# Weight-preparation buffers, operand loads and modulation gradients moved in a one-core adaLN transformer-block backward kernel

## The chip, the cores and the metric

The kernel runs on 1 core of one Trainium2 chip. The metric is device time in microseconds (us) of one launch. Five runs before the change gave 2850.62, 2851.59, 2852.38, 2853.69 and 2855.15 us; their median is 2852.38 us.

The core has a matrix engine (PE, with its own weight loads, PEld), a vector engine (DVE), an activation engine (ACT), a general engine (POOL, called GpSimd in the code) and a queue engine (SP, called `nc.sync`). SP and POOL also issue DMA transfers. All transfers run on the core's 16 DMA engines. Every engine takes its instructions strictly in order: an instruction that waits holds up all that are behind it on the same engine.

## The reference

The reference is the forward pass of one block and its gradients for ten tensors. S = 2048 rows, D = 512, F = 1792, 32 heads of 16.

```python
mod = (_silu(c) @ w_mod).reshape(c.shape[0], 6, 1, -1)     # sa, ca, ga, sb, cb, gb
h = _layernorm(x, axis=-1) * (1 + ca) + sa
x = x + ga * _A_ref(h, A_wqkv, A_wo)          # softmax attention
h = _layernorm(x, axis=-1) * (1 + cb) + sb
x = x + gb * _B_ref(h, B_w1, B_b1, B_w2, B_b2)   # squared-relu MLP
...
_out, _vjp = jax.vjp(_f, A_x, A_wqkv, A_wo, B_w1, B_b1, B_w2, B_b2, c, w_mod)
_grads = _vjp(grad_out)
```

The kernel returns the block's output (`out_0`), then the gradients of `A_x` (`out_1`), `A_wqkv` (`out_2`), `A_wo` (`out_3`), `B_w1`, `B_b1`, `B_w2`, `B_b2` (`out_4` to `out_7`), `c` (`out_8`) and `w_mod` (`out_9`). The last is 512 x 3072: six blocks of 512 columns, one for each of the six modulation vectors.

## The kernel before

The program has four stretches.

1. **Forward attention with the MLP beside it** (`phase_fwd`, L243): to about 1110 us.
2. **The last MLP chunk and the MLP's weight gradients** (`last_chunk`, L558). The weight gradients are generators that give one unit of work for each large matmul (`gen_dw1`, `gen_dw2`), driven by a `Background` object: `take(n)` runs n units, `until(mark)` runs up to a mark, `drain()` runs the rest. `gen_dw2` (L791) computes dW2 in 14 blocks, `ft` = 0 to 13, of 16 matmuls each. Block `ft` needs the transposed activations `a_blk` of that block, which SP loads with a transposing DMA (L802) from `aT_d` in HBM. `a_blk` has three buffers, and the load for block ft+2 is issued when block ft begins, so a load needs the buffer of the block three before. After each block DVE scales and reduces the result (L819, L822), POOL stores it (L820) and accumulates (L823). After block 7 the generator gives the mark "half", then does 16 matmuls for dB2 (L828), then blocks 8 to 13.
   At the mark "half" SP is given two other jobs, between the remaining `a_blk` loads:
   - `load_bwd` (L1102): 11 transfers ("pieces") that attention backward needs for its first head group: four of keys and values (128 KB each), four of QT and dOT (256 KB each), three of K, Q and dO (256 KB each).
   - `load_wmt` (L1108): four rounds, one for each 128 rows of `A_wqkv`. In a round SP loads the rows into `w_kt` (L1115, 384 KB), ACT scales them (L1116), and SP transposes them into `WmT` (L1118), the weights with which the last stretch computes dx. `w_kt` has one buffer, so the load of a round waits until the transpose of the round before has read it; the transpose waits for ACT, which waits for the load. `last_chunk` takes 13 units of dW2 at each of the eight stops of this generator.
3. **Attention backward** (`attn_bwd`, L1149): 1024 steps (8 head groups x 2 head pairs x 4 key chunks x 16 query blocks), 1250 to about 2707 us. A step does score matmuls (L1265), dP matmuls (L1218), exponentials on ACT (L1269), a product on DVE (L1223), and sends ds through a transposing DMA on SP (L1227, `dsT`) for the dQ matmuls (L1199).
4. **dx, the attention's weight gradients and the modulation gradients** (`phase6`, L1291): four generators, joined in one loop. `gen_a` (16 row tiles, 12 matmuls each) makes dx; its operand `dqT` comes through SP: `load_a` (L1323) issues three transposing DMAs (L1327) and one plain load (L1330) for a pair of row tiles, with two buffers, so a load waits until the pair two before is done. `gen_b` makes dWqkv: three column sums (L1355), then 12 blocks of 16 matmuls (L1368) into two PSUM buffers `g3ps`; DVE reads each result twice (L1373, L1376), and POOL stores it (L1374, two buffers `dwq`). `gen_c` makes dWo (L1393). `gen_p7` makes the gradients of `w_mod` and `c`, one vector `j` at a time in the order 3, 4, 5, 2, 0, 1: POOL loads 512 KB of `w_mod` into `wmod7` (L1434), PE broadcasts the vector (L1446), ACT copies it to `dm7` (L1448), DVE and ACT make the outer product `dwm7` (L1454, L1456), SP stores it (L1457, 512 KB), and DVE reduces against `wmod7` in four operations (L1460). `wmod7`, `dm7` and `dwm7` have one buffer each, so the load for the next j waits until this j's four reductions are done.
   The loop runs `gen_b` eight times, then rounds of c, b, a and, where its inputs are there, one j: j = 3, 4, 5 in rounds 1 to 3; j = 2 when c is done; j = 0 and 1 when b is done.

In stretches 1 to 3 the order on PE and SP is that of the code (`manual_schedule`, L142), and the order on the other engines comes from a planner that works on estimated times. In stretch 4 the planner orders all engines.

Of the kernel before, what the change touches and what calls it, by code (L numbers as in the profile page):

```python
# [8 lines left out]
BF16 = mybir.dt.bfloat16  # L9
# [9 lines left out]
P = 128  # L19
# [14 lines left out]
class Background:  # L34
# [13 lines left out]
    def next(self):  # L48
        while self.gens:
            r = next(self.gens[0], None)  # L50
            if r is not None:
                if isinstance(r, tuple):
                    self.mark = r[0]
                    self.seen.add(r[0])
                return r
            self.gens.pop(0)
        return None
# [30 lines left out]
class K:  # L88
# [469 lines left out]
    def last_chunk(self, bg, O_b, x0s):  # L558
# [5 lines left out]
        nc, io, mk, mps = self.nc, self.io, self.mk, self.mps  # L564
        D, F, H, NQ, ST, DT, FT, SC = self.D, self.F, self.H, self.NQ, self.ST, self.DT, self.FT, self.SC
        sc, s0, st0 = SC - 1, 512 * (SC - 1), 4 * (SC - 1)
        tm_v = lambda t: t.rearrange("(st p) d -> p st d", p=P)[:, st0:st0 + 4, :]
        tps = self.open_pool("tps", bufs=2, space=PSUM)
        e0 = self.open_pool("e0", bufs=1)
# [71 lines left out]
        fill = Background()  # L641
# [76 lines left out]
        next(g2)  # L718
        self.open_bwd()
        fill.until("half")  # L720
        self.load_bwd()
        for _ in self.load_wmt():
            fill.take(13)
        fill.drain()
        for name in ("dw2", "dw1", "e0", "dwps", "tps", "mps"):
            self.close_pool(name)

    def gen_dw1(self, sb, xh2):
# [370 lines left out]
                nc.vector.memset(m, 0.0)  # L1099
        self.qp = self.open_pool("p5q", bufs=1, side="right")  # L1100

    def load_bwd(self):  # L1102
        nc = self.nc
        self.T0, pieces = self.load_group(0)
        for (d, sr) in self.pair_pieces(0, 0) + pieces:
            nc.sync.dma_start(d, sr)

    def load_wmt(self):  # L1108

        nc, io = self.nc, self.io  # L1110
        D, DT = self.D, self.DT
        self.WmT = self.wp.tile([P, 3 * DT, D], BF16, name="WmT")
        for kt in range(DT):
            w = self.wp.tile([P, 3 * D], BF16, name="w_kt")
            nc.sync.dma_start(w[:], io["A_wqkv"][kt * P:(kt + 1) * P, :])  # L1115
            nc.scalar.activation(w[:], w[:], ACT.Copy, scale=self.opcaT[:, kt:kt + 1])  # L1116
            yield
            nc.sync.dma_start_transpose(self.WmT[:, :, kt * P:(kt + 1) * P], w[:])  # L1118
            yield

    def load_group(self, g):

# [168 lines left out]
    def phase6(self):  # L1291

        tc, nc, pp, io = self.tc, self.nc, self.pp, self.io
        S, D, H, ST, DT = self.S, self.D, self.H, self.ST, self.DT
# [8 lines left out]
        with ExitStack() as es:  # L1303
            sb = es.enter_context(tc.tile_pool(name="p6", bufs=1))
# [28 lines left out]
            def gen_a():  # L1333
                nxt = load_a(0)
                for s2 in range(0, ST, 2):
                    dqT, dx1 = nxt
                    if s2 + 2 < ST:
                        nxt = load_a(s2 + 2)
                    for k in range(2):
                        st = s2 + k  # L1340
                        pt = ps_a.tile([P, 512], F32, name="dxhps")
                        for nt in range(NT):
                            nc.tensor.matmul(pt[:], lhsT=dqT[:, nt // DT, k, nt % DT, :], rhs=WmT[:, nt, :],
                                             start=(nt == 0), stop=(nt == NT - 1))
                        dx0 = wk.tile([P, D], BF16, name="dx0")
                        self.ln_bwd_tile(wk, pt[:], xhat1[:, st, :], dx1[:, k, :], self.rstd1[:, st:st + 1], dx0[:])
                        nc.gpsimd.dma_start(out1_v[:, st, :], dx0[:])  # L1347
                        yield
# [57 lines left out]
            ga, gb, gc, g7 = gen_a(), gen_b(), gen_c(), self.gen_p7(sb, ob7, ps7)  # L1406
            want = next(g7)
            done = set()

            def run(name, gen):  # L1410
                if name not in done and next(gen, "done") == "done":
                    done.add(name)

            for _ in range(8):
                run("b", gb)
            while len(done) < 3 or want is not None:
                run("c", gc)
                run("b", gb)
                run("a", ga)
                if want is not None and (want in (3, 4, 5) or (want == 2 and "c" in done) or "b" in done):  # L1420
                    want = next(g7, None)
# [3 lines left out]
    def gen_p7(self, sb, ob, ps, order=(3, 4, 5, 2, 0, 1)):  # L1425
        tc, nc, pp, io = self.tc, self.nc, self.pp, self.io
        D, DT = self.D, self.DT
        wmod_v = io["w_mod"].rearrange("(kt p) n -> p kt n", p=P)
        dc_part = sb.tile([P, DT, 6], F32, name="dc_part")
        nc.gpsimd.memset(dc_part[:], 0.0)  # L1430
        for j in order:
            yield j
            wmod = ob.tile([P, DT, D], BF16, name="wmod7")
            nc.gpsimd.dma_start(wmod[:], wmod_v[:, :, j * D:(j + 1) * D])  # L1434
            cols = {0: self.dsa_col, 1: self.dca_col, 3: self.dsb_col, 4: self.dcb_col}
            if j == 2:
                dm = self.dga_bc
            else:
                if j == 5:
                    dg = self.dgb_acc  # L1440
                else:
                    dg = ob.tile([P, D], F32, name="dg7")
                    for kt in range(DT):
                        nc.vector.tensor_scalar(dg[:, kt * P:(kt + 1) * P], self.ident_f[:], cols[j][:, kt:kt + 1], None, ALU.mult)
                pt = ps.tile([P, 512], F32, name="bcps")
                nc.tensor.matmul(pt[:, :D], lhsT=self.ones_f[:], rhs=dg[:], start=True, stop=True)  # L1446
                dm = ob.tile([P, D], F32, name="dm7")
                nc.scalar.copy(dm[:], pt[:, :D])  # L1448
            if "dmod_bc" in self.dbg:
                nc.sync.dma_start(self.dbg["dmod_bc"][:, j * D:(j + 1) * D], dm[:])  # L1450
            o = ob.tile([P, DT, D], BF16, name="dwm7")
            for kt in range(DT):
                if kt % 2 == 0:
                    nc.vector.tensor_scalar(o[:, kt, :], dm[:], self.scT[:, kt:kt + 1], None, ALU.mult)  # L1454
                else:
                    nc.scalar.activation(o[:, kt, :], dm[:], ACT.Copy, scale=self.scT[:, kt:kt + 1])  # L1456
            nc.sync.dma_start(io["out_9"].rearrange("(kt p) n -> p kt n", p=P)[:, :, j * D:(j + 1) * D], o[:])  # L1457
            for kt in range(DT):
                junk = ob.tile([P, D], F32, name="junk7")
                nc.vector.scalar_tensor_tensor(junk[:], wmod[:, kt, :], 1.0, dm[:], ALU.mult, ALU.mult,  # L1460
                                               accum_out=dc_part[:, kt, j:j + 1])
        yield -1
        dcT = sb.tile([P, DT], F32, name="dcT")
        nc.vector.tensor_reduce(dcT[:], dc_part[:], axis=AX.X, op=ALU.add)
        nc.vector.tensor_tensor(dcT[:], dcT[:], self.dsiluT[:], ALU.mult)
        pt = ps.tile([P, 512], F32, name="bcps")
        nc.tensor.transpose(pt[:DT, :P], dcT[:], self.ident_f[:])
        dc_b = sb.tile([DT, P], BF16, name="dc_b")
        nc.vector.tensor_copy(dc_b[:], pt[:DT, :P])
        nc.sync.dma_start(io["out_8"].rearrange("o (t p) -> (o t) p", p=P), dc_b[:])  # L1470
# [73 lines left out]
```

The softmax here doesn't subtract the row's maximum and nothing guards it: scores larger than these inputs give would overflow.

## Time and profile before

One execution was profiled. It took 2850.62 us as a run, and its span from the first to the last instruction is 2848.8 us, so 1.8 us lie around the span.

| what | value |
|---|---|
| median of five runs | 2852.38 us |
| profiled execution, as a run | 2850.62 us |
| its span | 2848.8 us |
| PE busy | 2540.2 us, 89% of the span |
| ACT busy | 2214.7 us, 78% |
| DVE busy | 1786.4 us, 63% |
| POOL busy | 362.5 us, 13% |
| mean granted PE clock | 0.961 of full speed |
| first score matmul of attention backward (L1265) | 1250.18 us |
| last matmul of attention backward | about 2718 us |
| DMA share, 1200 to 1250 us | 0.97 |
| DMA share, 2700 to 2750, 2750 to 2800, 2800 to 2849 us | 0.94, 0.65, 0.76 |

How to read the views used below. A line of the timeline has the start in us, the length, the engine, the source line, the operation with output<-inputs, and the count of instructions merged into it. A bracket at its end gives how long the engine stood idle before it and what released it. SPq is SP as it issues DMAs; its length is the time for which the issue held the queue, not the transfer. A line of the waits view has who waited for whom, the total in us, the number of times, and the longest. The DMA share is the busy share of the 16 DMA engines and can pass 1.

### The profile page before, as it was taken

To read this page: it belongs to the slowest core of one execution; us is meant where nothing else is said; L and a number is where in the kernel's file an instruction comes from. 1 tells how busy PE (TensorE), PEld (TensorE's weight loads), DVE (VectorE), ACT (ScalarE), POOL (GpSimd) and SP (SyncE) were. 2 spreads that over 40 slices of the span, in tenths; PEclk is the share of its full clock that TensorE was granted. 3 is DMA by queue.
4 is the path that set the end of the run, shared out by engine and by line. 5 is a ranking of instruction groups with operands and counts; after the bars stand their busy time and mean duration, and the time that the engine had idled before them with its cause. 6 is when DMAs were issued, how large, how long until landed. Compare 5 with 4: busy or idle time off the path is not lost. (4 is left out here: it accounts for less than half of the span.)

```text
span 2848.8 us, 72467 instructions
## 1 busy us (share of the span) xinstructions
PE 2540.2 (89%) x30186; PEld 1214.3 (43%) x30186; DVE 1786.4 (63%) x2712; ACT 2214.7 (78%) x3376; POOL 362.5 (13%) x633
## 2 busy tenths in 40 slices
PE   5999799999999999978888888898988889888887
PEld 2555455555555545723333333333333333333343
DVE  4222423323312345658888888888988989889747
ACT  4999899999999975247778777777877878778623
POOL 2244202211311123420000000000000000000021
PEclk9999999999999999989999999999999999999899
DMA  4367743520531356989999999999999999999977
GB/s 150 86 148 161 166 78 100 122 53 29 144 86 45 100 151 176 196 194 201 212 196 204 207 200 210 196 203 204 195 208 200 201 207 199 208 201 207 213 192 187
DMA packets 1331345, 472.86 MB, mean 166 GB/s; under 512 B 1266470, under 2 KB 1293608, under 8 KB 1331016
## 3 DMA queue, kind: packets, MB, share of 16 engines
q1 hardware_dynamic: 1299816, 379.40, 72.6%
q0 software_dynamic: 29088, 86.21, 10.3%
q8 instruction: 236, 3.87, 0.5%
q10 hardware_dynamic: 2112, 2.62, 0.3%
q14 instruction: 93, 0.76, 0.1%
HBM read 83.30 MB, written 67.11 MB: 53 GB/s over the span
## 5 line engine op out<-in xcount | busy, mean ns | idle before, releaser
L1269 ACT ACTIVATE pu<-st 128x512 bf16<-128x512 f32 x2048 | 1109.0, 595 | 312.9 <-PE dp L1218 283.7
L1223 DVE TENSOR_TENSOR ds<-dp,pu 128x1024 bf16<-128x1024 f32 x1024 | 1213.2, 1219 | 195.7 <-PE dp L1218 155.8
L331 ACT ACTIVATE pu<-st 128x1024 bf16<-128x1024 f32 x1024 | 955.5, 1044 | 23.0 <-PE st L328 21.5
L328 PE MATMUL st<-QTm,KTq 128*128 128x512 bf16 x2048 | 608.7, 378 | 28.7 <-ACT pu L331 7.0
L293 PEld LDWEIGHTS <-pu 128*128 128x128 bf16 x8192 | 344.4, 96 | 246.4 <-issue 20.2
L1265 PE MATMUL st<-m,q 64*128 64x512 bf16 x1024 | 370.0, 402 | 19.0 <-ACT pu L1269 8.6
L1265 PE MATMUL st<-m,QTq 64*128 64x512 bf16 x1024 | 365.5, 398 | 15.9 <-ACT pu L1269 4.5
L1199 PEld LDWEIGHTS <-dsT 128*128 128x128 bf16 x8192 | 240.9, 97 | 309.4 <-DMA dsT<-ds 194.8
L1218 PE MATMUL dp<-m,q 64*128 64x512 bf16 x1024 | 371.9, 406 | 0.0
L1218 PE MATMUL dp<-m,dOTq 64*128 64x512 bf16 x1024 | 367.3, 402 | 0.0
L293 PE MATMUL accbank<-Vaug,pu 128*128 128x17 bf16 x8192 | 348.8, 171 | 13.6 <-DVE O L301 12.8
L328 PEld LDWEIGHTS <-KTq 128*128 128x128 bf16 x2048 | 194.4, 96 | 205.8 <-issue 140.5
L1199 PE MATMUL accq<-Kg,dsT 128*128 128x16 bf16 x4096 | 143.6, 171 | 81.6 <-DMA dsT<-ds 81.6
L1199 PE MATMUL accq<-q,dsT 128*128 128x16 bf16 x4096 | 144.3, 171 | 70.5 <-DMA dsT<-ds 70.2
L1434 POOL DMA_DIRECT2D wmod<-in_w_mod_dram x6 | 4.6, 774 | 1459.8 <-DVE kvT L1182 1453.6
L1179 PE MATMUL acckv<-ds,q 128*16 128x512 bf16 x1024 | 163.7, 402 | 0.0
L1179 PE MATMUL acckv<-pu,q 128*16 128x512 bf16 x1024 | 163.7, 402 | 0.0
L1179 PE MATMUL acckv<-ds,Qg 128*16 128x512 bf16 x1024 | 162.8, 400 | 0.7 <-DVE ds L1223 0.7
L1179 PE MATMUL acckv<-pu,dOg 128*16 128x512 bf16 x1024 | 162.9, 400 | 0.0
L1218 PEld LDWEIGHTS <-q 64*128 64x128 bf16 x1024 | 90.5, 94 | 111.4 <-issue 102.1
L1218 PEld LDWEIGHTS <-dOTq 64*128 64x128 bf16 x1024 | 89.4, 94 | 102.4 <-issue 93.6
L300 DVE RECIPROCAL rl<-accbank 128x4 f32<-128x4 f32 x128 | 22.9, 179 | 164.8 <-PE accbank L293 164.6
(309 smaller groups left out, 2372.3 us busy)
## 6 DMA issues: line engine op xcount, KB each, us to landing
KTq<-KTq_d POOLq DMA_DIRECT2D x24, 512.0 KB, 3.7
duT_d<-auT POOLq DMA_DIRECT2D x4, 1792.0 KB, 8.3
aT_d<-rT POOLq DMA_DIRECT2D x4, 1792.0 KB, 13.4
KTq_d<-KTq SPq DMA_DIRECT2D x32, 128.0 KB, 1.8
QTq_d<-ev_fm SPq DMA_DIRECT2D x32, 128.0 KB, 2.3
VTq_d<-vT POOLq DMA_DIRECT2D x4, 1024.0 KB, 6.2
O_d<-O POOLq DMA_DIRECT2D x4, 1024.0 KB, 5.4
m<-KTq_d SPq DMA_DIRECT2D x32, 128.0 KB, 3.6
```

The costliest lines, as they stand in the source:

```text
L293: nc.tensor.matmul(acc[:, a, sub, :], lhsT=pu[:, a, sub * P:(sub + 1) * P], rhs=Vaug[:, kb, h, :], start=(kb == 0 and a == 0 and sub == 0) ...
L300: nc.vector.reciprocal(self.rl[:, st0:st0 + 4, h], acc[:, a, :, DH])
L328: nc.tensor.matmul(stt[:, a, :], lhsT=KT[:, kb * P:(kb + 1) * P], rhs=QTm[2 * jp + a][:], start=True, stop=True)
L331: nc.scalar.activation(pu[:], stt[:], ACT.Exp, scale=self.scale)
L1179: nc.tensor.matmul(acckv[r:r + DH, :], lhsT=T[n][:, ib, col:col + DH], rhs=src[:, a, :], start=(ib == 0), stop=(ib == ST - 1))
L1199: nc.tensor.matmul(accq[:, ib, a, :], lhsT=dsT[:, (i * 2 + a) * 4 + sub, :], rhs=T["K"][:, 4 * c + sub, col:col + DH], start=(c == 0 and i ...
L1218: nc.tensor.matmul(dp[:, a, :], lhsT=T["dOT"][rd, ib * P:(ib + 1) * P], rhs=masked["VT"][2 * jp + a][rd, 512 * c:512 * (c + 1)], start=Tru ...
L1223: nc.vector.tensor_tensor(dsg[:, i], dp[:], pu[:], ALU.mult)
L1265: nc.tensor.matmul(stt[:], lhsT=T["QT"][rs, q], rhs=masked["KT"][2 * jp + a][rs, c0:c0 + 512], start=True, stop=True)
L1269: nc.scalar.activation(pu[:, a, :], stt[:], ACT.Exp, scale=self.scale)
L1434: nc.gpsimd.dma_start(wmod[:], wmod_v[:, :, j * D:(j + 1) * D])
```

## The change

The weight preparation `load_wmt` gets a pool of its own (`wkt`) with four buffers for `w_kt`. All four loads are issued first, with their ACT operations; the four transposes are a method of their own, `turn_wmt`. `load_bwd` goes; its 11 pieces are issued one at a time with 7 units of dW2 after each, and a transpose of `WmT` after every third piece, the fourth after the last piece. Counted out from "half", SP's order becomes: four `w_kt` loads; pieces 0, 1, 2; `a_blk` 10; transpose 0; pieces 3, 4; `a_blk` 11; piece 5; transpose 1; piece 6; `a_blk` 12; pieces 7, 8; transpose 2; piece 9; `a_blk` 13; piece 10; transpose 3.

In `phase6` the vectors j = 3, 4, 5 move from the first three rounds to three places among the eight `gen_b` steps: after the second, third and fourth block of dWqkv (`gen_b` steps k = 4, 5, 6; steps 0 to 2 are the column sums). The store of `out_9` moves from SP to POOL for all six j.

```diff
         fill.until("half")
-        self.load_bwd()
-        for _ in self.load_wmt():
-            fill.take(13)
+        ws = self.load_wmt(self.open_pool("wkt", bufs=1))
+        self.T0, pieces = self.load_group(0)
+        pieces = self.pair_pieces(0, 0) + pieces
+        for n, (d, sr) in enumerate(pieces):
+            nc.sync.dma_start(d, sr)
+            fill.take(7)
+            if n % 3 == 2 and ws:
+                self.turn_wmt(*ws.pop(0))
+        for w in ws:
+            self.turn_wmt(*w)
         fill.drain()
-        for name in ("dw2", "dw1", "e0", "dwps", "tps", "mps"):
+        for name in ("wkt", "dw2", "dw1", "e0", "dwps", "tps", "mps"):
             self.close_pool(name)
...
-    def load_wmt(self):
+    def load_wmt(self, sb):
...
+        ws = []
         for kt in range(DT):
-            w = self.wp.tile([P, 3 * D], BF16, name="w_kt")
+            w = sb.tile([P, 3 * D], BF16, name="w_kt", bufs=DT)
             nc.sync.dma_start(w[:], io["A_wqkv"][kt * P:(kt + 1) * P, :])
             nc.scalar.activation(w[:], w[:], ACT.Copy, scale=self.opcaT[:, kt:kt + 1])
-            yield
-            nc.sync.dma_start_transpose(self.WmT[:, :, kt * P:(kt + 1) * P], w[:])
-            yield
+            ws.append((kt, w))
+        return ws
+
+    def turn_wmt(self, kt, w):
+        self.nc.sync.dma_start_transpose(self.WmT[:, :, kt * P:(kt + 1) * P], w[:])
...
-            for _ in range(8):
+            for k in range(8):
                 run("b", gb)
+                if k > 3 and want in (3, 4, 5):
+                    want = next(g7, None)
...
-            nc.sync.dma_start(io["out_9"].rearrange("(kt p) n -> p kt n", p=P)[:, :, j * D:(j + 1) * D], o[:])
+            nc.gpsimd.dma_start(io["out_9"].rearrange("(kt p) n -> p kt n", p=P)[:, :, j * D:(j + 1) * D], o[:])
```

More of the change, by code (lines that the diff above doesn't have):

```diff
@@ L1100, in open_bwd @@
         self.qp = self.open_pool("p5q", bufs=1, side="right")
[L1102 to L1106, printed above, removed]
-    def load_wmt(self):
+    def load_wmt(self, sb):
         nc, io = self.nc, self.io
```

## The prediction

> **What bounds the kernel now.** I read the page's busy shares first (PE 89%, ACT 78%: no engine is full over the whole span), then the waits of the two stretches that the change touches, then their timelines. All times are us from the span's start.
>
> The waits from 1205 to 1256, the end of dW2, show one long PE wait, on `a_blk`, and SP held by the chain of the single `w_kt` buffer:
>
> ```profile
> PE dps L816 <- DMA a_blk<-aT_d: 11.9, 3, 9.6
> ACT w_kt L1116 <- DMA w_kt<-in_A_wqkv_dram: 23.2, 3, 8.4
> ...
> SPq L1118 <- ACT w_kt L1116: 10.7, 3, 7.1
> ```
>
> The timelines of PE, SP and ACT there (three queues, in this order):
>
> ```profile
> 1214.80 7.07 PE L816 MATMUL dps<-g_tm,a_blk 128*128 128x512 bf16 x32
> 1231.49 9.26 PE L816 MATMUL dps<-g_tm,a_blk 128*128 128x512 bf16 x32 [9.62 <-DMA a_blk<-aT_d]
> 1241.40 3.63 PE L816 MATMUL dps<-g_tm,a_blk 128*128 128x512 bf16 x16 [0.65 <-DMA a_blk<-aT_d]
> 1246.62 3.63 PE L816 MATMUL dps<-g_tm,a_blk 128*128 128x512 bf16 x16 [1.59 <-DMA a_blk<-aT_d]
> 1254.25 0.58 PE L1265 MATMUL st<-m,q 64*128 64x512 bf16 x1 [3.47 <-ACT pu L1269]
> ...
> 1217.12 0.34 SPq L1115 DMA_DIRECT2D w_kt<-in_A_wqkv_dram  x1
> 1224.90 1.47 SPq L1118 DMA_TRANSPOSE WmT<-w_kt  x1
> 1226.47 2.34 SPq L802 DMA_TRANSPOSE a_blk<-aT_d  x1
> 1239.62 2.89 SPq L802 DMA_TRANSPOSE a_blk<-aT_d  x1
> ...
> 1251.19 1.57 ACT L1116 ACTIVATE w_kt<-w_kt,opcaT 128x1536 bf16<-128x1536 bf16 x1 [6.92 <-DMA w_kt<-in_A_wqkv_dram]
> 1253.60 1.08 ACT L1269 ACTIVATE pu<-st 128x512 bf16<-128x512 f32 x2 [0.84 <-DMA out_dram<-dw]
> ```
>
> Read it so: blocks 8 and 9 end at 1221.87. Block 10's operand is issued only at 1226.47, because SP stood from 1217.46 to 1224.90 at the first transpose, waiting for load and scaling. PE idles 9.62, and the next 32 matmuls take 9.26 instead of 7.07. dW2 ends at 1250.25; the first exponential of attention backward starts 3.35 later. Attention then runs on dependent steps to 2718, so what starts earlier here ends earlier.
>
> At the other end, `phase6`, PE is dense from 2743 to 2815 (in 2750 to 2800 it is busy 50.00 of 50.00), and then waits for `dqT`. PE and SP:
>
> ```profile
> 2742.82 3.61 PE L1368 MATMUL g3ps<-dv_t,m 128*128 128x512 bf16 x16 [1.60 <-DVE junk L1376]
> 2815.74 2.76 PE L1343 MATMUL dxhps<-WmT,dqT 128*128 128x512 bf16 x12 [1.12 <-DMA dqT<-dq_t]
> 2826.32 6.39 PE L1343 MATMUL dxhps<-WmT,dqT 128*128 128x512 bf16 x21 [4.37 <-DMA dqT<-dq_t]
> 2833.92 5.35 PE L1343 MATMUL dxhps<-WmT,dqT 128*128 128x512 bf16 x24 [0.45 <-DMA dqT<-dq_t]
> ...
> 2813.77 0.42 SPq L1457 DMA_DIRECT2D out_dram<-dwm  x1
> 2814.65 2.19 SPq L1327 DMA_TRANSPOSE dqT<-dk_t  x1
> 2819.27 4.57 SPq L1327 DMA_TRANSPOSE dqT<-dq_t  x1
> 2824.58 0.40 SPq L1457 DMA_DIRECT2D out_dram<-dwm  x1
> ```
>
> **The change, part by part.**
>
> *dW2's tail.* Floor: from 1221.87 four blocks at 3.45 each (the spacing of DVE's L819 in undisturbed blocks) end at 1235.7: 14.5 less than 1250.25, if no operand is late. What is late next is SP itself. It reaches "half" at 1210.69. Up to the end of issuing `a_blk` 13 it now has four `w_kt` loads at 0.34 plus a gap (0.40), ten pieces at 0.58 (11 took 6.43 before), three transposes at 1.45 and four `a_blk` at 2.73 (mean of the four before): 1.6 + 5.8 + 4.4 + 10.9 = 22.7, so 1233.4. Blocks 10 and 12 before began 2.7 and 2.55 after their issue ended; with 2.7 block 13 starts at 1236.1 and ends at 1239.6. That is **10.6 gained**, and block 10's 9.62 is gone: its issue ends at 1210.69 + 1.6 + 1.7 + 2.7 = 1216.7, five before PE is ready. Its `a_blk` buffer, block 7's, is free at 1211.55; the later ones, 8 to 10, at 1218.45, 1221.9 and about 1225, also before SP comes to them. The transposes now find their ACT work done: four scalings of 1.57 on an ACT that was idle from 1185 to 1223.
> The pessimistic end: every `a_blk` issue takes 3.80, the longest of the 14 (4.3 more), and the last block starts 4.11 after its issue, as block 13 did before: it ends at 1245.3, gain 5.0. DMA is the reason to keep this end: its share was already 0.97 in 1200 to 1250, and the same bytes now move in some 28 instead of 40. I stay nearer the middle since the engines had gaps there (two of over 1 while ACT scaled).
>
> *ACT's wait at the start of attention.* I count nothing for it. Fourth scaling and store release the first exponential 0.84 apart; with the scaling away, the store of block 13 is left: DVE 0.69, POOL 0.3 + 0.56, landing 1.77 after PE's end, the same 3.35. If it went too, 3.35 more.
>
> *Pieces, `wkt`'s place.* The pieces are the same 11 transfers; keys and values go early, the last (dO) after 1233, needed first some 6 after attention's start. Costs nothing unless SP is later than 1239. The 12 KB of `wkt` are later used by `dsT`, first written at 1260.57 before, 10 after attention's start, when the last transpose is long issued: nothing.
>
> *Vectors 3, 4, 5 earlier.* PE's work is moved, not changed: three pairs of L1446, 0.86 each. Two of them now stand before the fourth block, whose 1.60 wait for DVE they cover: -1.6. DVE gets per vector two products (0.48) and four reductions (0.76), 4.0, in a stretch where it idled between dWqkv blocks (2.9 per 3.45). What is queued behind: POOL's load of the next `wmod7` waits for the last reduction, and behind it stand the stores of dWqkv; on DVE the reductions wait for that load, and behind them stands L1376, which frees `g3ps`. Vector 3's reductions end about 2740.5; POOL's issue 0.77; landing 4.6 at the median, 10.3 at the longest (the one of 2706.75). PE needs the fourth block's buffer at about 2750.7. With 4.6 vector 4's reductions end at 2748.9: no stall. With 10.3 they end at 2754.6, with L1376 2755.3: 4.6 stall, and the same again for vector 5, 9.2 in all. The nearest row is the store of a dWqkv block issued at 2733, 8.2; DMA is a little freer by 2741, so I take 7: 1.3. Sum -1.6 + 1.3 = **-0.3**, between -1.6 and +7.6.
>
> *`out_9` through POOL.* SP loses six issues of 0.41; only the last two stand in the tail where SP is late: 0.8. The store of 2813.77 put 512 KB ahead of the transposes of rows 12 and 13 in the same queue, at the 400 GB/s seen for plain loads about 1.3; these took 9.2 instead of 4.0 (rows 8 and 9). I take **-2.1**. Ends: all three waits for `dqT` gone, -5.9; or nothing gained and POOL's two issues of 0.77 ahead of the last `out_1` stores, +1.5.
> [...]
>
> *Sum:* -10.6 - 0.3 - 2.1 = -13.0. The profiled execution would go from 2850.62 to 2837.6 (span 2835.8). The median shown lies 1.76 above that execution: 2852.38 - 13.0 = **2839.4**. Ends added up: 2852.38 - 22.0 = 2830.4 and 2852.38 + 4.1 = 2856.5.
>
> **Rivals.** No change that a measurement of this kernel can tell is about 0.2%, 5.7 us.
>
> 1. *Transposing DMAs become the bound of dW2.* For: share 0.97, issues up to 3.80. Against: idle gaps, and 11 of the 14 `a_blk` never made PE wait. Gain 5.0 there, 2.4 in `phase6`: 2845.0. Chance 0.17.
> 2. *`phase6` gives it back in part.* Both `wmod7` loads land after 10.3 (+7.6) and the tail gains nothing: -10.6 + 7.6 + 0 = -3.0, 2849.4. For: 4 MB of `O_tm` and `dx1b` stand in POOL's queue from 2719. Chance 0.13, "same".
> 3. *Slower: DVE blocked by POOL's queue.* The planner puts all reductions of vectors 4 and 5 ahead of the dWqkv blocks' reads, and each load comes 10.3 late: vector 4 done 2754.6, vector 5 at 2754.6 + 0.8 + 10.3 + 3.0 = 2768.7, L1376 1.4 later. PE, out of buffers at 2750.7, stands 19.4. With nothing won in the tail: -10.6 - 1.6 + 19.4 = +7.2, 2859.6. It decides from a stall of about 18. For: DVE is strictly in order and has waited for this load (3.07 at 2824). Against: in rounds 1 to 3 the planner interleaved both kinds. Chance 0.11.
> 4. *The early start is not kept*, attention being limited by `dsT` transfers (6.3 of PE's wait at its end): it would need slack inside 1024 dependent steps; no row shows it. Inside the chance of rival 2.
>
> **How the numbers follow.** Forecast as summed, 0.59, own range 2832 to 2843 (dW2 gain 8 to 14, `phase6` -6 to 0); rival 1 0.17; rivals 2 and 4 0.13; rival 3 0.11. Faster: 0.59 + 0.17 = 0.76; same 0.13; slower 0.11. The range 2830 to 2852 takes in the forecast, rival 1 and rival 2, and leaves out rival 3 and some below.
>
> **What would show it.** Right: PE's wait on `a_blk` in dW2 falls from 11.9 to under 4, L1116 comes four times in a row before 1225, the first L1265 starts near 1240, and the first exponential still waits for `out_dram<-dw` with about 3.4. In `phase6`, `out_dram<-dwm` stands on POOL, the wait of L1368 for L1376 is below 2, `dqT` waits sum to 3 to 5, and L1327 for rows 12 and 13 takes under 7. Wrong: `a_blk` issues above 3.5 and three waits of 2 to 3 (rival 1); DVE idle before L1460 for `wmod` by 5 or more with PE idle before L1368 (rivals 2, 3); attention backward (first L1265 to last L1199, 1468.3 now) longer by more than 3, for which I have no mechanism.

## The result, and the profile after

The changed kernel takes 2859.94 us (median of 31 runs, 2853.45 to 2869.34) against 2853.12 us for the kernel before (median of 58 runs, 2844.09 to 2868.95). The ratio is 1.0021, with a 95% interval of 1.0013 to 1.0029: slower by about 6 us, where 13 us faster was forecast. The profiled execution of the changed kernel took 2853.45 us, with a span of 2851.7, which is the lowest of its runs. So the two profiled spans differ by only 2.9 us.

I cut both traces at the same events. "Tail" runs from the first dB2 matmul to the first score matmul of attention backward, "attention" from there to the end of the last dQ matmul, "last" from there to the end of the last dx matmul, "rest" from there to the end of the span.

| stretch, us | before | after | difference |
|---|---|---|---|
| forward, up to its last exponentials | – | – | -3.9 |
| from there to dB2 | 172.6 | 172.8 | +0.2 |
| tail | 38.84 | 37.09 | -1.75 |
| attention | 1468.25 | 1466.80 | -1.45 |
| last | 120.84 | 130.14 | +9.30 |
| rest | 9.53 | 10.11 | +0.58 |
| span | 2848.8 | 2851.7 | +2.9 |

The forward pass has the same code in both kernels, so its -3.9 is scatter between executions. Without it the rows add up to +6.9, close to what the medians say. Almost all the loss is in the last stretch, where -2.4 was forecast, and the gain of 10.6 in the tail has shrunk to 1.75.

**The tail.** The timeline of the changed kernel (PE, then SP, then ACT):

```profile
1211.01 7.07 PE L823 MATMUL dps<-g_tm,a_blk 128*128 128x512 bf16 x32
1219.59 3.63 PE L823 MATMUL dps<-g_tm,a_blk 128*128 128x512 bf16 x16 [1.51 <-DMA a_blk<-aT_d]
1227.35 6.29 PE L823 MATMUL dps<-g_tm,a_blk 128*128 128x512 bf16 x16 [4.13 <-DMA a_blk<-aT_d]
1234.24 3.63 PE L823 MATMUL dps<-g_tm,a_blk 128*128 128x512 bf16 x16 [0.60 <-DMA a_blk<-aT_d]
1241.09 3.63 PE L823 MATMUL dps<-g_tm,a_blk 128*128 128x512 bf16 x16 [3.23 <-DMA a_blk<-aT_d]
1248.88 0.37 PE L1269 MATMUL st<-m,q 64*128 64x512 bf16 x1 [3.63 <-ACT pu L1273]
...
1206.75 1.99 SPq L1117 DMA_DIRECT2D w_kt<-in_A_wqkv_dram  x4
1210.84 6.21 SPq L809 DMA_TRANSPOSE a_blk<-aT_d  x1
1220.24 3.64 SPq L809 DMA_TRANSPOSE a_blk<-aT_d  x1
1227.58 4.64 SPq L809 DMA_TRANSPOSE a_blk<-aT_d  x1
1236.04 2.89 SPq L809 DMA_TRANSPOSE a_blk<-aT_d  x1
...
1211.83 5.97 ACT L1118 ACTIVATE w_kt<-w_kt,opcaT 128x1536 bf16<-128x1536 bf16 x4 [30.79 <-DMA w_kt<-in_A_wqkv_dram]
1248.23 2.15 ACT L1273 ACTIVATE pu<-st 128x512 bf16<-128x512 f32 x4 [30.43 <-DMA out_dram<-dw]
```

SP no longer stands at the first transpose of `WmT`: the four loads and the four scalings come in a row, as the change intends. But the issue of `a_blk` 10, forecast at 2.73, holds SP for 6.21, and the three after it take 3.64, 4.64 and 2.89. So PE waits for `a_blk` four times instead of three: 1.51 + 4.13 + 0.60 + 3.23 = 9.47 in place of 9.62 + 0.65 + 1.59 = 11.86. The one long wait has become several short ones.

The table by stretches of 10 us (stretch, length, busy time of PE, PEld, DVE, ACT and POOL, granted clock, DMA share, GB/s), first of the changed kernel, then of the kernel before:

```profile
1220.00:1230.00 10.00, 5.87 (x22) 2.27 (x21) 1.29 (x2) 0.00 (x0) 3.73 (x5) 0.80 1.12 246
1230.00:1240.00 10.00, 7.26 (x27) 2.62 (x25) 2.58 (x4) 0.00 (x0) 2.91 (x4) 0.86 1.16 235
```

```profile
1220.00:1230.00 10.00, 1.87 (x9) 0.67 (x7) 1.29 (x2) 1.57 (x1) 4.09 (x6) 0.79 0.73 207
1230.00:1240.00 10.00, 8.51 (x30) 3.46 (x31) 1.29 (x2) 1.57 (x1) 1.66 (x2) 0.70 1.03 194
```

Before, the DMA engines had a hole here (share 0.73). After, there is none: the share stays at 1.12 and 1.16, and PE waits for DMA.

The 4.13 wait has a second price: the 16 matmuls behind it took 6.29 instead of 3.63. Behind the waits of 1.51 and 3.23 they still took 3.63. Two kernels of the experiments below (e3, then e5) show that the length of the wait alone does not decide:

```profile
1223.13 5.30 PE L823 MATMUL dps<-g_tm,a_blk 128*128 128x512 bf16 x16 [2.33 <-DMA a_blk<-aT_d]
```

```profile
1238.91 5.31 PE L823 MATMUL dps<-g_tm,a_blk 128*128 128x512 bf16 x16 [2.02 <-DMA a_blk<-aT_d]
```

In the changed kernel the granted clock was 0.50 from 1226 to 1232, at the end of the 4.13 wait and in the matmuls behind it, and 1.00 around the waits of 1.51 and 3.23; in e3 its mean from 1220 to 1230, around the 2.33 wait, was 0.83. What decides is not shown.

**The last stretch.** The timeline of the changed kernel (POOL, DVE, PE):

```profile
2711.76 0.94 POOL L1321 DMA_DIRECT2D O_tm<-O_d  x1 [1464.16 <-PE accq L1203]
2723.86 0.57 POOL L1378 DMA_DIRECT2D out_dram<-dwq  x1 [8.33 <-DVE dwq L1377]
2725.35 0.75 POOL L1440 DMA_DIRECT2D wmod<-in_w_mod_dram  x1 [0.92 <-issue]
...
2739.26 0.69 DVE L1466 SCALAR_TENSOR_TENSOR junk<-wmod,dm 128x512 f32<-128x512 bf16 x1 [10.03 <-DMA wmod<-in_w_mod_dram]
2743.38 0.55 DVE L1450 TENSOR_SCALAR dg<-ident_f,dcb_col 128x128 f32<-128x128 f32 x1
...
2743.98 2.07 PE L1452 MATMUL bcps<-dg,ones_f 128*128 128x512 f32 x2 [10.50 <-DVE dg L1450]
```

Its waits in this stretch (who waits for whom: total, times, longest):

```profile
DVE junk L1466 <- DMA wmod<-in_w_mod_dram: 13.2, 4, 10.0
...
PE bcps L1452 <- DVE dg L1450: 10.5, 1, 10.5
```

And the same load in the kernel before, on POOL's timeline:

```profile
2706.75 0.79 POOL L1434 DMA_DIRECT2D wmod<-in_w_mod_dram  x1 [1453.62 <-DVE kvT L1182]
2719.00 0.91 POOL L1317 DMA_DIRECT2D O_tm<-O_d  x1 [11.46 <-PE accq L1199]
```

Before, the first load of `w_mod` (vector 3) is issued 12 us ahead of the 4 MB of `O_tm` and `dx1b`. After, it stands behind them and behind the first store of dWqkv in the same queue: issued at 2725.35, it lands 13.8 later (before 10.3). DVE stands 10.03 at vector 3's first reduction. Vector 4's diagonal `dg` (L1450) is queued behind that reduction on DVE, PE's broadcast of vector 4 waits for `dg`, and PE, also in order, has the rest of dWqkv behind that broadcast: 10.50 us in which PE does nothing, where it stood 1.60 before (L1368 for L1376). That is the loss.

Nothing in the diff touches this load. What moved it is a place in SBUF. Before, `w_kt` (3 KB per partition) was a tile of the pool `p5w`. With a pool of its own, `p5w` shrank by 3072 bytes, and its neighbours moved up by as much. In the built programs' addresses per partition, before and after:

```
          before              after
p5q       152512..166848      155584..169920
p5c       166848..183264      169920..186336
p5w       183264..198624      186336..198624
phase6's pool with wmod7, dg7: 168832..183168 in both
```

So `wmod7` (168832 to 172928) lay before over `p5c` alone, which is free once the last scores are done; the load waited for `kvT`. After, it also lies over `p5q`, which the last dQ matmuls read. So the load may start only some microseconds later, and in the order that the planner makes for stretch 4 it then stands behind the other loads. In all nine kernels below that keep those 3 KB in `p5w` (the kernel before among them) POOL issues it ahead of `O_tm`; in the three that don't and leave the load to POOL (after, e1, e7) it issues it behind.

### The profile page after: what moved, and what is told of

It is laid out like the page before. It is cut to its first block, busy times and chain, and to the rows that moved or that the text cites. A ratio compares the mean times of both kernels' runs of the same rounds, so it can differ in the third digit from the quotient of the medians.

```text
span 2851.7 us, 72466 instructions
## 1 busy us (share of the span) xinstructions
PE 2538.6 (89%) x30186; PEld 1212.0 (43%) x30186; DVE 1787.4 (63%) x2712; ACT 2214.4 (78%) x3376; POOL 366.2 (13%) x639
## 3 DMA queue, kind: packets, MB, share of 16 engines
q0 software_dynamic: 29952, 89.36, 10.7%
## 4 chain that ended last, share of the span: by engine, by line
DMA 35%; PE 17%; DVE 4%; ACT 3%; issue 2%; POOL 0%; SPq 0%; DVEq 0%; POOLq 0%; ACTq 0%
DMA dsT<-ds 33%; PE st L1269 5%; DVE ds L1227 3%; PE accq L1203 3%; ACT pu L1273 3%; PE acckv L1183 2%; PE dps L823 1%; PE g3ps L1372 1%; PE dxhps L1347 1%; DMA a_blk<-aT_d 1%; PE dp L1192 1%; DMA out_dram<-dw 1%; PE pps L622 0%; DMA wmod<-in_w_mod_dram 0%; PE gps L1397 0%
## 5 line engine op out<-in xcount | busy, mean ns | idle before, releaser
L1227 DVE TENSOR_TENSOR ds<-dp,pu 128x1024 bf16<-128x1024 f32 x1024 | 1213.5, 1220 | 196.2 <-PE dp L1222 156.0
```

The source lines that it names most:

```text
L1227: nc.vector.tensor_tensor(dsg[:, i], dp[:], pu[:], ALU.mult)
```

## The experiments

Two things were to be explained. For the last stretch, one theory says that the displaced pool and the early vectors together make the wait: the first puts the load late, the second puts somebody behind it. Its rivals: the early vectors alone do it, or the stores of `out_9` in POOL's queue do it. For the tail, one theory is that plain loads ahead in SP's queue hold up the transposing DMAs; the rival is that the transposes of `WmT` themselves compete with those of `a_blk`.

The stretches of all kernels, one profiled execution each. "dW to dx" is the last stretch counted from the first dWqkv block. Where no interval is given, the kernel was run once, and its total says little, since single runs of the kernel before spread over 25 us.

| kernel | median, us | ratio (95%) | tail | last | dW to dx |
|---|---|---|---|---|---|
| before | 2853.12 | – | 38.84 | 120.84 | 112.0 |
| after | 2859.94 | 1.0021 (1.0013 to 1.0029) | 37.09 | 130.14 | 122.5 |
| e1_dw2_only | 2852.39 | 0.9994 (0.998 to 1.0009) | 42.22 | 123.41 | 113.3 |
| e2_phase6_only | 2854.43 | 1.0006 (0.9991 to 1.0021) | 40.46 | 122.58 | 112.4 |
| e3_after_hold | 2852.43 | 1.0002 (0.9984 to 1.0019) | 38.16 | 122.30 | 112.3 |
| e4_wkt_early | 2858.39 | 1.0013 (0.9995 to 1.0031) | 28.68 | 128.74 | 119.2 |
| e5_no_wkt | 2853.73 | – | 29.34 | 122.75 | 112.4 |
| e6_load3_by_act | 2847.37 | – | 40.59 | 123.16 | 113.0 |
| e7_store_by_sp | 2862.94 | – | 38.94 | 135.31 | 126.0 |
| e8_wmt_by_pe | 2847.47 | 0.998 (0.9968 to 0.9992) | 36.96 | 118.12 | 108.8 |
| e9_no_load | 2855.56 | – | 33.38 | 122.46 | 113.8 |
| e10_no_turn | 2844.54 | – | 31.72 | 122.78 | 112.7 |
| e11_wmt_by_pe_spread | 2846.16 | 0.9975 (0.9956 to 0.9995) | 31.57 | 118.74 | 109.6 |

**Each half alone.** e1 is the changed kernel with `phase6` as it was before:

```diff
-            for k in range(8):
+            for _ in range(8):
                 run("b", gb)
-                if k > 3 and want in (3, 4, 5):
-                    want = next(g7, None)
...
-            nc.gpsimd.dma_start(io["out_9"]...
+            nc.sync.dma_start(io["out_9"]...
```

> Only the dW2 part of the change; vectors 3 to 5 stay in the rounds and out_9 is stored by SP, as before. Stretches, before / changed kernel: dW2 tail (first dB2 matmul to first score matmul) 38.8 / 37.1; attention 1468.3 / 1466.8; last stretch (end of last dQ matmul to end of last dx matmul) 120.8 / 130.1. Layout theory (the 3 KB that w_kt leaves in p5w move the attention operands p5q over the place of wmod7, so that vector 3's w_mod load waits for the last dQ matmul and goes behind the 4 MB of O_tm and dx1b): the load is late here too, but nobody needs it before 2750, so the last stretch is 119 to 122; dW2 tail 36 to 38; total about 2 us faster than before, ratio 0.999. Rival (the dW2 part alone slows the last stretch): 125 to 131 there, ratio 1.001 to 1.003.

e2 is the kernel before with the other half:

```diff
-            for _ in range(8):
+            for k in range(8):
                 run("b", gb)
+                if k > 3 and want in (3, 4, 5):
+                    want = next(g7, None)
...
-            nc.sync.dma_start(io["out_9"]...
+            nc.gpsimd.dma_start(io["out_9"]...
```

> Only the phase6 part: vectors 3 to 5 early and out_9 stored by POOL; dW2 tail and the place of w_kt as before. Layout theory: vector 3's w_mod load stays ahead of the 4 MB, no wait of L1446 for dg above 2 us, last stretch 117 to 121 (before 120.8), total 0 to 3 us faster than before, ratio 0.999 to 1.000. Rival (early vectors overload DVE and POOL wherever the load stands): the wait is there, 8 to 11 us, last stretch 128 to 131, ratio 1.003.

Neither half can be told from no change (0.9994 and 1.0006), and in neither is the last stretch long (dW to dx 113.3 and 112.4). So the loss needs both. The sizes were missed in part: e1's tail was expected at 36 to 38, and the last stretches (123.41 and 122.58) lie above the 122 and 121 that were expected at most. In e1 the load of vector 3 is late as well, issued at 2738.50 where `O_tm` went out at 2721.84. But with the vectors in their late places nothing PE needs soon is queued behind it. In e2 the load stands in front (2708.30 against 2719.28) and PE waits 2.28 for `dg`.

**The place.** e3 is the changed kernel with 3 KB put back into `p5w`, so that all pools lie where they lay before:

```diff
         self.WmT = self.wp.tile([P, 3 * DT, D], BF16, name="WmT")
+        hold = self.wp.tile([P, 3 * D], BF16, name="hold")
+        nc.vector.memset(hold[:, 0:2], 0.0)
```

> The whole change, with a tile of 3 KB left in p5w (one memset of two columns), so that all places in SBUF are those of before. Layout theory: the load of vector 3 stands ahead of O_tm, the wait of 10.5 us goes, last stretch 117 to 121, dW2 tail unchanged at 36 to 38, total 2 to 5 us faster than before, ratio 0.998 to 0.9995. Rival (early vectors themselves): last stretch 128 to 131, ratio 1.002 as for the changed kernel.

Its timeline (SP, POOL, PE):

```profile
1214.07 6.49 SPq L809 DMA_TRANSPOSE a_blk<-aT_d  x1
...
2706.07 0.79 POOL L1442 DMA_DIRECT2D wmod<-in_w_mod_dram  x1 [1454.69 <-DVE kvT L1188]
2717.38 0.91 POOL L1323 DMA_DIRECT2D O_tm<-O_d  x1 [10.52 <-PE accq L1205]
...
2743.52 1.12 PE L1454 MATMUL bcps<-dg,ones_f 128*128 128x512 f32 x2 [2.26 <-DVE dg L1452]
```

With an unused tile of 3 KB the load is back in front, the 10.50 wait is 2.26, and dW to dx is 112.3 instead of 122.5 (112.0 before; the last stretch, 122.30, is still above the 117 to 121 expected). The place is a cause, and the whole of this loss goes with it. The median (ratio 1.0002) fits, though the intervals of e3 and of the changed kernel overlap, so the time alone would not prove it. The tail is as before (38.16), and the first `a_blk` issue takes 6.49 here too.

**The load by another queue, and the store by SP.** e6 is the changed kernel, with the load of vector 3 issued by ACT; e7 is the changed kernel with the stores of `out_9` on SP again.

```diff
-            nc.gpsimd.dma_start(wmod[:], wmod_v[:, :, j * D:(j + 1) * D])
+            (nc.scalar if j == 3 else nc.gpsimd).dma_start(wmod[:], wmod_v[:, :, j * D:(j + 1) * D])
```

> The changed kernel with one edit: vector 3's w_mod load is issued by ACT's queue instead of POOL's. The 4 MB of O_tm and dx1b still move at that time. Theory of the POOL queue (the load waits its turn behind the 4 MB): it lands 4 to 6 us after its issue, PE's wait of L1446 for dg falls from 10.5 to under 4, last stretch 121 to 125. Rival (the DMA engines are full, any queue is as slow): lands after 10 or more, wait 7 to 11, last stretch 127 to 131.

```diff
-            nc.gpsimd.dma_start(io["out_9"]...
+            nc.sync.dma_start(io["out_9"]...
```

> The changed kernel with out_9 stored by SP again, vectors 3 to 5 still early, places in SBUF as changed. Layout theory: the wait of 10.5 us stays at 9 to 12, last stretch 128 to 132; in the tail PE's waits for dqT are within 1.5 of the 5.5 with POOL, since only the issue moves. Rival (the stores in POOL's queue hold its loads): the wait falls under 5.

The DMA issues of e6 at 2712 (tile, queue, KB each, us from issue to landing), and below them the timeline of e7 (POOL, DVE, PE):

```profile
O_tm<-O_d POOLq DMA_DIRECT2D x1, 1024.0 KB, 8.4
wmod<-in_w_mod_dram ACTq DMA_DIRECT2D x1, 512.0 KB, 3.8
```

```profile
2731.84 0.75 POOL L1440 DMA_DIRECT2D wmod<-in_w_mod_dram  x1 [0.92 <-issue]
...
2746.59 0.69 DVE L1466 SCALAR_TENSOR_TENSOR junk<-wmod,dm 128x512 f32<-128x512 bf16 x1 [10.87 <-DMA wmod<-in_w_mod_dram]
...
2751.32 2.08 PE L1452 MATMUL bcps<-dg,ones_f 128*128 128x512 f32 x2 [11.35 <-DVE dg L1450]
```

In e6 the displaced pools stay, the load is issued at 2712.73 beside `O_tm` and lands after 3.8; PE's wait is 0.38 and dW to dx 113.0. So with the place as it is, the late landing of this load was the means. Issue time and queue both changed; which of them shortened the transfer was not separated. The order behind `O_tm` is not the only thing that makes the load slow: in the nine kernels that issue it ahead of `O_tm`, it landed after 4.5 to 10.7. In e7 the loss stays, at 11.35 (its last stretch, 135.31, is even longer than the 132 expected at most), so the loss does not need the stores on POOL.

**What held the transposing DMAs in the tail.** Three kernels built on e3 leave out work. Their expectations say what; in each the loads, the transposes or both are replaced by a fill or a copy on an engine.

e9, no loads of `w_kt`:

```diff
-            nc.sync.dma_start(w[:], io["A_wqkv"][kt * P:(kt + 1) * P, :])
-            nc.scalar.activation(w[:], w[:], ACT.Copy, scale=self.opcaT[:, kt:kt + 1])
+            nc.scalar.activation(w[:, :DT], self.opcaT[:], ACT.Copy)
+            nc.vector.memset(w[:, DT:], 0.01)
```

> The whole change with the held 3 KB, and the four w_kt loads left out: w_kt is filled by ACT and DVE, the four transposes stay, so out_1 is not the gradient. Theory that the plain loads ahead of them hold SP's transposing DMAs: the issue of a_blk 10 falls from 6.5 to 2.3 to 3.0, PE's waits for a_blk after the first dB2 matmul from 9.6 to 3 to 6, dW2 tail from 38.2 to 31 to 35. Rival (transposes alone set the pace, each waiting for the one before): a_blk 10 still above 5, tail 36 to 39.

e10, no transposing DMAs of `WmT`:

```diff
-        self.nc.sync.dma_start_transpose(self.WmT[:, :, kt * P:(kt + 1) * P], w[:])
+        self.nc.scalar.copy(self.WmT[:, 3 * kt:3 * kt + 3, :], w[:].rearrange("p (a b) -> p a b", a=3))
```

> The whole change with the held 3 KB, and the four transposing DMAs of WmT left out: ACT copies the scaled rows into WmT as they are, the four loads stay, so out_1 is not the gradient. Theory that the plain loads ahead hold the first transposing DMA: a_blk 10 is still issued in 5.5 to 6.5, but a_blk 11 to 13 stand 1.5 to 5 earlier, waits 2 to 6, dW2 tail 31 to 35. Rival (transposes alone set the pace): waits 0 to 3, tail 28 to 31.

e5, neither:

```diff
-            nc.sync.dma_start(w[:], io["A_wqkv"][kt * P:(kt + 1) * P, :])
-            nc.scalar.activation(w[:], w[:], ACT.Copy, scale=self.opcaT[:, kt:kt + 1])
+            nc.scalar.activation(w[:, 0:2], self.opcaT[:, 0:2], ACT.Copy)
+            nc.gpsimd.memset(self.WmT[:, :, kt * P:(kt + 1) * P], 0.01)
...
-        self.nc.sync.dma_start_transpose(self.WmT[:, :, kt * P:(kt + 1) * P], w[:])
+        pass
```

> The whole change with the held 3 KB, and the w_kt work left out: no load of A_wqkv rows, no scaling, no transpose; POOL fills WmT with a constant, so out_1 is not the gradient. The stretch from the first dB2 matmul to the first score matmul was 38.2 with the work and a floor of 3.45 x 7 + 3.4 = 27.6 without any wait. DMA theory (the stretch is as long as its bytes take): 1.5 MB of loads and 1.5 MB of transposes are gone, 3.9 + 5.4 of DMA time at the rates seen for such transfers alone, so the stretch falls to 28 to 31. Queue theory (SP's order holds the a_blk loads, not the bytes): the four loads at the head go too, so it falls as well, but the 11 pieces still stand between, and a_blk 11 to 13 stay late: 32 to 35.

The issue of `a_blk` 10 in e9, and the first two issues in e10, on SP's timeline:

```profile
1214.09 3.28 SPq L809 DMA_TRANSPOSE a_blk<-aT_d  x1
```

```profile
1215.24 6.33 SPq L809 DMA_TRANSPOSE a_blk<-aT_d  x1
1222.75 4.04 SPq L809 DMA_TRANSPOSE a_blk<-aT_d  x1
```

Without the plain loads ahead the first issue takes 3.28; with them, and without the other transposes, 6.33. In e5, without both, it takes 3.41; in all seven kernels with the four loads and three pieces ahead (after, e1, e3, e6, e7, e8, e10) it takes 5.84 to 6.61. So it is the loads that hold the first transposing DMA of the queue. The later waits go with the sum of the traffic: the tail is 38.16 with everything (e3), 33.4 without the loads, 31.7 without the transposes, 29.3 without both. All three lie below the shortest of five tails with everything (37.1 to 42.2, further below); the differences between the three are within that spread. So both theories hold a part of it. The sizes were missed in part: e9's first issue was expected at 3.0 at most, and e10's waits for `a_blk` sum to 6.8, not 2 to 6. These three tails are bounds rather than prices: in e5 the fills by POOL ran ahead of the tail, and the stretch up to dB2 grew to 180.9 (e3 174.2); in e10 it was 178.8, and why is open.

**The same bytes earlier.** e4, on e3, issues the loads and three of the transposes ahead of "half", one per 24 units:

```diff
+        ws = []
+        for kt, w in self.load_wmt(self.open_pool("wkt", bufs=1)):
+            ws.append((kt, w))
+            fill.take(24)
+            if kt:
+                self.turn_wmt(*ws.pop(0))
         fill.until("half")
-        ws = self.load_wmt(self.open_pool("wkt", bufs=1))
```

> As the kernel with the held 3 KB, and the four w_kt loads come one by one ahead of the mark half, 24 units of dW1 and dW2 apart, three of the four transposes too; after half only the 11 pieces and one transpose remain between the a_blk loads. Queue theory (SP's transposing DMAs are held while the plain loads ahead of them in its queue drain: 6.2 us for a_blk 10, 4.6 for a_blk 12): a_blk issues after half fall to 2.3 to 3.6, PE's waits for a_blk sum to 0 to 4 instead of 9.5, dW2 tail 25 to 31, total 8 to 15 us faster than before, ratio 0.995 to 0.997. Rival (all DMA engines are full and the bytes only move to other waits): waits on du_blk or a_blk ahead of half grow by what is won, total 2 to 5 us faster, as the kernel with the held 3 KB.

PE's timeline in e4, ahead of the tail and in `phase6`:

```profile
1187.81 16.09 PE L828 MATMUL dps<-g_tm,a_blk 128*128 128x512 bf16 x64 [4.63 <-DVE junk L792]
1207.98 12.22 PE L828 MATMUL dps<-g_tm,a_blk 128*128 128x512 bf16 x48 [4.08 <-DMA a_blk<-aT_d]
...
2746.07 2.08 PE L1457 MATMUL bcps<-dg,ones_f 128*128 128x512 f32 x2 [4.59 <-DVE dg L1455]
```

The tail falls to 28.68, and the stretch ahead of it grows from 174.2 (e3) to 184.1: a wait of 4.08 for `a_blk` and one of 4.63 for DVE stand there, and the total (1.0013) is no better, where 8 to 15 us were expected. The bytes have been moved, not hidden. Its last stretch is also longer than e3's (128.74), with a 4.59 wait for `dg`, although the load of vector 3 stands in front of `O_tm` at 2706.47. The late load doesn't explain that. DVE's timeline does in part; before, e3 and e4, the read of the third dWqkv block:

```profile
2741.41 0.75 DVE L1373 SCALAR_TENSOR_TENSOR dwq<-g3ps,opcaT,t 128x512 bf16<-128x512 f32 x1 [4.89 <-DMA out_dram<-dwq]
```

```profile
2741.02 0.75 DVE L1379 SCALAR_TENSOR_TENSOR dwq<-g3ps,opcaT,t 128x512 bf16<-128x512 f32 x1 [1.80 <-DMA out_dram<-dwq]
```

```profile
2743.57 0.75 DVE L1382 SCALAR_TENSOR_TENSOR dwq<-g3ps,opcaT,t 128x512 bf16<-128x512 f32 x1 [4.13 <-DMA out_dram<-dwq]
```

In all three, DVE stands for the store of an earlier dWqkv block, because `dwq` has two buffers; in e3 and e4 vector 4's `dg` is queued behind that. The stores landed after 7.7 in e3 and 10.0 in e4 (medians of the two issued from 2730 to 2736). So e4's 6.9 more from dW to dx are 2.3 of the wait for `dg`, some 3 of slower matmuls behind it, and 1.7 more of waits for `dqT`. Why the stores landed later stays open.

**PE in place of the transposing DMAs.** If transposing DMAs and loads collide, PE can transpose `w_kt` itself. e8 is e1 with the place kept and twelve groups of PE transposes, their results copied by ACT:

```diff
+        def turn_w(kt, w):
+            for t in range(3):
+                turn(w[:, t * D:(t + 1) * D], DT, self.WmT[:, t * DT:(t + 1) * DT, kt * P:(kt + 1) * P], "scalar")
...
-            if n % 3 == 2 and ws:
-                self.turn_wmt(*ws.pop(0))
+            if n > 1 and n % 2 == 0 and ws:
+                turn_w(*ws.pop(0))
         for w in ws:
-            self.turn_wmt(*w)
+            turn_w(*w)
```

> A version meant to beat both: the dW2 part with the held 3 KB, phase6 as before (late vectors, stores by SP), and WmT transposed by PE and ACT (12 groups of four 128x128 transposes and one copy out of PSUM) instead of by the four transposing DMAs, which takes 1.5 MB off the DMA engines. DMA theory: dW2 tail 31 to 35 (before 38.8, changed 37.1), last stretch 119 to 122, total 4 to 9 us faster than before, ratio 0.997 to 0.9985. Queue theory: tail 35 to 38, ratio 0.999 to 1.000.

PE in e8:

```profile
1223.82 0.58 PE L576 MATMUL tp<-ident,w_kt 128*128 128x128 bf16 x4 [4.45 <-ACT WmT L577]
...
1246.59 3.63 PE L828 MATMUL dps<-g_tm,a_blk 128*128 128x512 bf16 x16 [0.22 <-DMA a_blk<-aT_d]
```

The waits for `a_blk` are gone but for 0.22. A wait for ACT has come instead: the copies out of PSUM stand behind the four scalings on ACT (4.45). The tail, 36.96, is that of the rival (35 to 38). e11 therefore issues one load per piece, spreads the twelve groups, and shares the copies between DVE and ACT:

```diff
+            if n < DT:
+                kt, w = next(lw)
+                ws += [(kt, w, t) for t in range(3)]
             nc.sync.dma_start(d, sr)
-            fill.take(7)
-            if n > 1 and n % 2 == 0 and ws:
+            fill.take(4)
+            if n > 2:
                 turn_w(*ws.pop(0))
+            fill.take(3)
         for w in ws:
             turn_w(*w)
+            fill.take(5)
```

> The version with WmT transposed by PE, mended where its trace showed PE waiting: the four w_kt loads one ahead of each of the first four pieces, the 12 groups of transposes one at a time between units of dW2 from the fourth piece on, copied out of PSUM by DVE and ACT in turn. phase6 as before, held 3 KB. Floor 27.6 plus 12 groups at 0.38 is 32.2. Theory (with 1.5 MB less of transposing DMA the a_blk loads keep up): dW2 tail 32 to 35, waits for a_blk under 2, total 5 to 10 us faster than before, ratio 0.9965 to 0.998. Rival (DMA is full anyway): tail 36 to 39, ratio 0.999 to 1.

PE in e11:

```profile
1232.71 1.46 PE L833 MATMUL dps<-g_tm,a_blk 128*128 128x512 bf16 x3 [2.60 <-DMA a_blk<-aT_d]
...
1242.77 3.63 PE L833 MATMUL dps<-g_tm,a_blk 128*128 128x512 bf16 x16 [0.20 <-DMA a_blk<-aT_d]
```

The tail is 31.57, with 2.8 of waiting for `a_blk` (under 2 expected), though PE does more work in it than before. At 2846.16 us e11 takes 0.9975 of the time of the kernel before (0.9956 to 0.9995): a version that beats both, the kernel before by about 7 us. e8 is within its interval (0.998, 0.9968 to 0.9992). Their last stretches are also the shortest of all (118.12 and 118.74, against 120.84 before), although `phase6` and the places of its pools are those of the kernel before: PE's 1.60 wait is absent, since DVE stood 2.89 and 3.25 for the stores of `dwq` instead of 4.89, and the waits for `dqT` sum to 4.5 and 5.1 instead of 5.9. Why these transfers landed earlier is open. So of e11's gain only the shorter tail (-7.3 in one execution each) can be put down to its edit, and there PE's transposes and the loads one by one were changed together; e8, with PE's transposes alone, has no tail that can be told from the others.

## Why the prediction was wrong, point by point

*dW2's tail, -10.6; measured -1.75 in one execution, and nothing that can be told from scatter.* Five kernels with the changed order (after, e1, e3, e6, e7) have tails of 37.1, 42.2, 38.2, 40.6 and 38.9, mean 39.4; two with the old order have 38.8 and 40.5, mean 39.7. So even the "pessimistic end" of 5.0 was too good. The step that failed is "`a_blk` at 2.73 (mean of the four before)", which made SP's work up to `a_blk` 13 some 22.7 long. The issues took 6.21, 3.64, 4.64 and 2.89: 17.4 where 10.9 was counted; with 3.0 more for the loads, pieces and gaps between them, the issue of `a_blk` 13 ended 32.2 after "half" (1206.75 to 1238.93) and not 22.7. Block 10's issue ended at 1217.05, 1.03 before PE was ready and not five, and with its landing 1.51 too late. The 2.73 came from rows with few plain loads ahead, and was carried to a place behind 1.5 MB of them and three pieces. Rival 1, transposing DMAs that become the bound, came nearest: its sign, issues above 3.5, was seen. But e9 and e10 put a part on the plain loads, which it does not name, and its size was too small, because its issue of 3.80 was the longest of 14 without such loads ahead.

*ACT's wait at the start of attention, 3.35, counted at nothing.* Right: the first exponential still waits for `out_dram<-dw`, and starts 3.51 after the last dW2 matmul ends (1244.72 to 1248.23).

*Pieces, `wkt`'s place, counted at nothing.* This is the step that turned no change into a loss: e3, with the place kept, takes 2852.43 us (ratio 1.0002), so the missing gain of the tail alone would have ended there. I looked at what later uses the 12 KB of the new pool (`dsT`) and not at what the 3 KB taken out of the old one move. Measured: 10.50 of PE's wait, and 10.5 more from the first dWqkv block to the last dx. With the place kept (e3) the wait is 2.26, and 0.3 is left of the 10.5.

*Vectors 3, 4, 5 earlier, -0.3.* Of its parts, the -1.6 is not seen even with the load in front: dW to dx is 112.3 and 112.4 in e3 and e2, 112.0 before. The 1.60 wait stands before the fifth block, not the fourth (64 matmuls are ahead of it), and came from a store: DVE stood 4.89 until a dWqkv block was stored, and freed `g3ps` late. That long wait, and not room between the blocks, is most of DVE's idle time there; the "2.9 per 3.45" is a misreading, between the first two blocks DVE's row has 1.36. In e3 and e2 DVE still stands 1.80 and 1.82 for that store, vector 4's `dg` is queued behind it, and PE waits about 2.3 for `dg`. The price of 1.3 was set on the loads of vectors 4 and 5; these cost DVE waits of 0.45 to 2.5 in the kernels with these vectors, and 4.74 once in e6, where PE waited 0.4. The stall came a vector earlier, with "Vector 3's reductions end about 2740.5" as the step: they ended at 2742.8, and the broadcast of vector 4 stood behind them. That the broadcast of the next vector, in PE's own order ahead of the dWqkv blocks, waits for DVE was the chain I didn't follow.

*`out_9` through POOL, -2.1.* Wrong; here it is worth nothing. The `dqT` waits sum to 5.5 in the changed kernel, 5.9 before. Over the kernels they are 5.5 to 7.5 with stores by POOL (after, e2 to e6, e9, e10), and 4.5 to 7.0 with stores by SP (before, e1, e7, e8, e11). The transposes of rows 12 and 13 take 8.7, where 9.2 was measured before and under 7 forecast. The step that failed is the 1.3 for "512 KB ahead of the transposes in the same queue": here the waits stayed, whoever issued the 512 KB. A small loss came with it: from the last dx matmul to the end, most kernels with stores by POOL take 10.1, those with stores by SP 9.46 to 9.60. The cause of that 0.5 is open.

*The rivals.* The time came out on rival 3's (2859.6). That is luck: its sum took off 10.6 of gain in the tail that did not come and added a stall of 19.4. Its mechanism is the nearest: DVE stands at a reduction for a load in POOL's queue, and PE runs dry. But the wait was one of 10.5, at vector 3's load, and not two at those of vectors 4 and 5; and its point of decision, "a stall of about 18", assumed the 10.6 gain in the tail. With that gone, 10.5 were enough. Of the signs that the prediction named, it was those of rivals 1 and 3 that came: `a_blk` issues above 3.5 with waits spread over several blocks, and DVE idle for `wmod` by more than 5, though PE then stood ahead of a broadcast (L1452) and not of a dWqkv block. Rival 4 is not seen: attention took 1466.8 against 1468.3.

## What to carry to other kernels

A tile taken out of one pool moves the pools beside it, and what then shares a place with what decides which load may go first: compare the addresses of both builds, and follow each first load to the reader it now has to wait for (here 3072 bytes put an issue of 2706.75 to 2725.35). An engine that runs in order turns one late load into a stall of whoever's operand is queued behind the waiting instruction (10.03 us of DVE here, and with it 10.50 of PE), so moving work earlier has to be checked against the load it needs and against everything that will stand behind it. And a stall whose waiting transfer is replaced by the same bytes in less time can come back in pieces, as here (11.86 us in three waits, then 9.47 in four); moving the transposes from the DMA engines to PE and spreading the loads (e11) gained what reordering the transfers did not (tail 31.57, against 37.09).

## What the runs showed of the hardware that I had not expected

- The issue of a transposing DMA held its queue for 5.84 to 6.61 behind 1.5 MB of plain loads and three pieces (seven kernels), and for 3.28 and 3.41 without those loads (e9, e5). The 14 issues of the kernel before have a median of 2.57 and a longest of 3.80.
- A 512 KB load issued by POOL behind 4 MB of its own queue (10.8 and 12.5 after the last of them was issued) landed after 13.8 and 14.7 (after, e7); issued by ACT at the start of the same 4 MB it landed after 3.8, while the 1 MB of `O_tm` took 8.4 (e6). With none of the 4 MB ahead it landed after 4.5 to 10.7 in nine kernels, so more than the order in the queue is at work.
- From 1220 to 1240 the changed kernel had a DMA share of 1.12 and 1.16 while only 246 and 235 GB/s moved. From 1217 to 1222 the kernel before moved 367 to 402 GB/s at a share of 1.04 to 1.07.
- In the changed kernel slower matmuls followed a wait of 4.13 (6.29 for 16), but not waits of 3.23 or 1.51 (3.63); in e3 and e5 they followed waits of 2.33 and 2.02 (5.30 and 5.31).
